# Another recording order for the first 1084 steps of a two-layer attention and feed-forward kernel

## The chip, the cores and the metric

The kernel runs on one core of a Trainium2 chip. The core has five engines, each with an instruction queue of its own that it works through in order: TensorE (PE in the profile; PEld are its weight loads), VectorE (DVE), ScalarE (ACT), GpSimd (POOL) and SyncE (SP), which here does nothing but issue DMAs. Engines wait for each other by semaphores. The metric is the device time of one execution, in microseconds.

## The reference

The program applies four layers to x (2048 tokens of 640 features), all with the same weights: attention, feed-forward, attention, feed-forward, each on a layer norm of x and each added to x.

```python
x = A_x
x = x + _A_ref(_layernorm(x, axis=-1), A_wq, A_wk, A_wv, A_wo, A_beta)
x = x + _B_ref(_layernorm(x, axis=-1), B_w1, B_w2)
x = x + _A_ref(_layernorm(x, axis=-1), A_wq, A_wk, A_wv, A_wo, A_beta)
x = x + _B_ref(_layernorm(x, axis=-1), B_w1, B_w2)
```

The attention has 32 heads of 20 features and works in 4 segments of 512 tokens. Within a segment it is causal softmax attention; beside it each head reads a memory matrix M, the sum of phi(k)^T v over the earlier segments, with phi(t) = t+1 for t > 0 and exp(t) otherwise. A gate per head mixes the two, and wo projects the result. The feed-forward is relu(x w1) w2 with 1728 hidden features.

## The kernel before

All weights and x stay on the core. The work is cut by layer and segment, and each kind of work is a Python generator (a stream) that yields steps one by one: an instruction, or a few that belong together, for one engine, with what they wait for. 39 streams are added at the end of the kernel, numbered from 0 in this order: scores, exps, causal, apply, free_v, turn_pair, divide, turn_o, two out_proj, two ln_b, fill, spill, combine, two phi_, two mem_read, turn_k, mem_write, first_sums, four first_one, first_ln_b, proj_ln, proj_first, two proj_one, proj_v, ffn, ffn_rest, store, warm_pe, consts, loads, late_loads. Some streams spawn small ones, mostly the copy that empties a PSUM bank.

The steps of segment 0, in the terms that are used below:

- `loads` brings x and the weights; `first_one` normalizes the first four tiles of 128 tokens and transposes them on TensorE; `proj_first`, `proj_one` (q and k, 512 columns a step) and `proj_v` (320 columns) project. A projection is five steps into one PSUM bank, at L774 or, in four column quarters, at L777. A copy (L981, L982, L1036) on VectorE or ScalarE empties the bank.
- `spill` (L1070) writes q and k to DRAM, `fill` (L1117) reads them back into `pad` with one head per group of 32 rows; four fills make the `pad` of two groups of four heads. The first pair comes straight from `stg` (L1097).
- `scores` (L1301) multiplies q and k in row groups. One step is a round, called SC0, SC1 and so on here; five rounds are the scores of eight heads. Each round ends in two exponentials on ScalarE (`exps`, L1365), which empty its banks; `causal` (L1377, GpSimd) masks them.
- `apply` multiplies the probabilities with v: at L1397 in column quarters (a value product), for groups 6 and 7 by token, in eight whole steps each (L1436). `turn_pair` transposes the result by DMA (L817), `divide` normalizes it, `out_proj` follows.
- `phi_` makes the features for the memory (L1144, L1146, L1147), `mem_write` (L1238) and `mem_read` (L1180) update and read it; `proj_ln` and `ln_b` are the layer norms (statistics at L795), whose results a DMA transposes (L817); `ffn` and `ffn_rest` (L1572) are the feed-forward; `late_loads` brings the later x, wo, w1 and w2.

Several of these TensorE steps exist in two forms, whole or in four column quarters. Going from row groups, whole or quarters to another of the three is called a change of form here.

What sets the order is a list scheduler (`Sched.run`). It keeps an estimated time for every engine, takes of all streams the step that could start first, shifted by priorities, by margins and by the table SHIFT, and records it: the instruction goes to the end of its engine's queue. So the order of recording is the program order of each queue. The scheduler also chooses the engine of a PSUM copy and the form of a TensorE step. 5068 steps are recorded.

## Time and profile before

| | before |
|---|---|
| median of 3 runs | 551.33 us (550.27 to 551.43) |
| profiled execution: span from the first to the last instruction | 549.3 us |
| TensorE busy | 539.8 us (98%) |
| VectorE busy | 427.8 us (78%) |
| ScalarE busy | 406.0 us (74%) |
| GpSimd busy | 195.7 us (36%) |
| mean granted TensorE clock | 1.000 |

The profile gives the profiled execution's time as its span; the runs' times also hold what lies around it, 2.0 us by the median. The page lists busy time by engine, the span in 40 slices, the DMA queues, the chain of work that ended last, and groups of instructions by line. Matmuls are pipelined: a matmul's duration in the profile is longer than the distance to the next one. A row of the timeline reads: start in us, length, engine, line, operation, result and operands, shapes, count, and in brackets idle time before it and what ended it.

### The profile page before, as it was taken

The numbers are of one execution on the slowest core, as the hardware profiler recorded it, in microseconds if no ns is written. First come the engines' busy times: TensorE is split into PE (matmuls) and PEld (weight loads), VectorE is DVE, ScalarE is ACT, GpSimd is POOL, SyncE is SP. The second block draws the span as 40 slices with busy tenths as digits, with TensorE's granted clock in tenths as the row PEclk, the third lists the DMA queues.
The fourth block names the chain that finished last, engine by engine and source line by source line (L and its number), as shares of the span: only waits on it lengthen the run. The fifth ranks groups of instructions, "written<-read, shape, count | busy, mean of one in ns | idle before, by whom it ended". The sixth has DMA issues, their size and how long they took to land.

```text
span 549.3 us, 20483 instructions
## 1 busy us (share of the span) xinstructions
PE 539.8 (98%) x9025; PEld 305.5 (56%) x9025; DVE 427.8 (78%) x1067; ACT 406.0 (74%) x516; POOL 195.7 (36%) x305
## 2 busy tenths in 40 slices
PE   7999999999999999999999999999999999999997
PEld 6543464455554546646556555564646654757656
DVE  4899999898999989898778858997899788417102
ACT  5699899789888987788888867897778787350130
POOL 5255444333453334443433423433333333201000
PEclk9999999999999999999999999999999999999999
DMA  8699979715384175438384743336246511541201
GB/s 270 165 198 253 245 158 223 221 44 116 89 165 98 40 180 77 75 68 120 47 212 93 116 116 93 58 69 104 50 139 130 117 32 22 106 63 33 71 2 51
DMA packets 133325, 62.20 MB, mean 113 GB/s; under 512 B 112116, under 2 KB 123124, under 8 KB 133236
## 3 DMA queue, kind: packets, MB, share of 16 engines
q1 hardware_dynamic: 132672, 60.36, 51.5%
q8 instruction: 71, 1.16, 0.9%
q10 hardware_dynamic: 564, 0.53, 0.4%
q14 instruction: 18, 0.15, 0.1%
HBM read 20.56 MB, written 12.85 MB: 61 GB/s over the span
## 4 chain that ended last, share of the span: by engine, by line
PE 88%; ACT 6%; DVE 2%; DMA 2%; SPq 1%; issue 0%
PE ps L774 35%; PE ps L777 35%; PE ps L1301 8%; PE ps L1397 6%; ACT PT L1365 5%; PE ps L1180 2%; DMA x_sb<-in_A_x_dram 1%; PE ps L1572 1%; PE ps L1238 1%; DMA pad<-scr 1%; SPq L602 1%; DVE xn_tok L841 0%; SPq L612 0%; DVE stats L795 0%; DVE x_sb L1614 0%; DVE o_sb L1491 0%
## 5 line engine op out<-in xcount | busy, mean ns | idle before, releaser
L1365 ACT ACTIVATE PT<-ps 128x1024 bf16<-128x1024 f32 x320 | 308.9, 1028 | 59.3 <-PE ps L1301 57.6
L1377 POOL TENSOR_SCALAR_AFFINE_SELECT PT<-PT 128x512 bf16<-128x512 bf16 x256 | 169.3, 679 | 241.1 <-ACT PT L1365 241.0
L777 PE MATMUL ps<-xnT,w_r 128*32 128x512 bf16 x1256 | 76.0, 379 | 0.0
L777 PE MATMUL ps<-w_r,hT 128*32 128x320 bf16 (+1 forms) x1764 | 67.8, 295 | 0.0
L1614 DVE TENSOR_TENSOR x_sb<-x_sb,ps 128x320 bf16<-128x320 bf16 (+1 forms) x65 | 30.7, 474 | 43.6 <-PE ps L777 38.7
L1301 PE MATMUL ps<-pad 20*128 20x512 bf16 (+3 forms) x1024 | 63.4, 301 | 1.2 <-ACT PT L1365 0.7
L774 PE MATMUL ps<-w_r,hT 128*128 128x320 bf16 x404 | 64.2, 300 | 0.0
L795 DVE BATCH_NORM_STATS2 stats<-x_sb 128x6 f32<-128x320 bf16 x124 | 55.0, 478 | 3.8 <-DMA x_sb<-in_A_x_dram 3.0
L777 PEld LDWEIGHTS ps<-w_r,hT 128*32 128x32 bf16 x1764 | 45.2, 97 | 12.6 <-issue 1.4
L1595 ACT ACTIVATE hT<-ps 128x512 bf16<-128x512 f32 x50 | 29.9, 599 | 29.0 <-PE ps L777 25.6
L774 PE MATMUL ps<-xnT,w_r 128*128 128x512 bf16 x206 | 50.8, 380 | 0.0
L774 PEld LDWEIGHTS ps<-w_r,hT 128*128 128x128 bf16 x404 | 37.6, 98 | 19.4 <-issue 4.9
L1301 PEld LDWEIGHTS ps<-pad 20*128 20x128 bf16 x1024 | 17.9, 92 | 52.9 <-issue 24.5
L777 PEld LDWEIGHTS ps<-xnT,w_r 128*32 128x32 bf16 x1256 | 31.6, 97 | 27.8 <-issue 2.0
L1519 DVE TENSOR_TENSOR x_sb<-x_sb,ps 128x320 bf16<-128x320 bf16 x64 | 29.7, 478 | 20.4 <-PE ps L777 16.0
L811 POOL TENSOR_TENSOR rstd<-lnU,mhalf 128x2 f32<-128x2 f32 (+2 forms) x27 | 21.1, 782 | 63.5 <-DVE lnU L807 60.4
L1407 DVE CAST otu<-ps 128x512 bf16<-128x512 f32 x52 | 35.6, 685 | 9.1 <-PE ps L1397 8.2
L1397 PE MATMUL ps<-PT,v_aug 128*21 128x128 bf16 (+3 forms) x896 | 40.3, 300 | 0.0
L1594 DVE TENSOR_SCALAR hT<-ps 128x512 bf16<-128x512 f32 x54 | 36.5, 681 | 1.7 <-PE ps L774 0.7
L1491 DVE TENSOR_TENSOR o_sb<-otk,rden 128x320 bf16<-128x320 bf16 x62 | 34.8, 588 | 0.5
L981 DVE CAST stg<-ps 128x512 bf16<-128x512 f32 (+1 forms) x37 | 24.7, 669 | 12.5 <-PE ps L774 6.3
L1146 ACT ACTIVATE stg<-stg 128x512 bf16<-128x512 bf16 x50 | 31.7, 635 | 2.0 <-DVE rtmp L1144 1.8
(118 smaller groups left out, 731.5 us busy)
## 6 DMA issues: line engine op xcount, KB each, us to landing
pad<-scr SPq DMA_DIRECT2D x124, 80.0 KB
scr<-stg SPq DMA_DIRECT2D x34, 256.0 KB, 2.5
out_dram<-x_sb SPq DMA_DIRECT2D x15, 160.0 KB, 1.9
w_r<-in_B_w_dram SPq DMA_DIRECT2D x10, 216.0 KB, 4.0
w_r<-in_B_w_dram SPq DMA_DIRECT2D x13, 160.0 KB, 2.8
x_sb<-in_A_x_dram SPq DMA_DIRECT2D x10, 160.0 KB, 3.2
scr<-w_r SPq DMA_DIRECT2D x5, 256.0 KB, 4.2
wv_r<-in_A_wv_dram SPq DMA_DIRECT2D x1, 800.0 KB, 9.7
```

Of the source, the lines that this page charges most:

```text
L774: return e.matmul(view(dst.ap, b), a, b, start=(k == 0), stop=(k == last))
L777: return e.matmul(view(dst.ap[rows], b), part, b, start=(k == 0), stop=(k == last))
L795: tk = yield dve(320, 1, lambda e, c2=c2: e.bn_stats(stats6[:, t, c2, :], x_sb[:, t, c2 * 320:(c2 + 1) * 320]), xt)
L1146: te = yield act(512, lambda e, q=q: e.activation(q, q, ACT.Exp), [tr] + p, psum=False)
L1301: fns.append([(lambda e, z=z, j=j, hh=hh, N=N, o=o, sl=sl, q=hh % 2: e.matmul(slot.ap[:, q, o:o + N], sl.ap[32 * hh:32 * hh + DH, z, 0, 12 ...
L1365: tx = yield act(1024, lambda e, dst=dst, src=src: e.activation(dst, src, ACT.Exp, scale=SCALE), sc + pw)
L1377: tm = yield pool(600.0, lambda e, reg=reg: e.affine_select(out=reg, in_=reg, pattern=[[0, 4], [1, 128]], compare_op=ALU.is_ge, fill=0.0, ...
L1397: fns.append((lambda e, OD, j=j, hh=hh: e.matmul(OD.ap[32 * hh:32 * hh + DH + 1, 128 * j:L], VAUG[vx(a, s)][:, j, 4 * g + hh, :], pt.ap[:, ...
L1407: te = yield evac(L, 1, lambda e: e.tensor_copy(dst, OD.ap), lambda e: e.activation(dst, OD.ap, ACT.Copy), [tk] + OTU[0].tks)
L1491: to = yield dve(320, 1, lambda e, z=z, dst=dst: e.tensor_tensor(dst, av[:, z, :, :, 0:DH], rd.ap[:, z].to_broadcast([128, NJ, 4, DH]), AL ...
L1594: th = yield evac(512, 1, lambda e: e.tensor_scalar(hT[:, dc, :], bk.ap[:, :], 0.0, None, ALU.max), lambda e: e.activation(hT[:, dc, :], b ...
L1614: ta = yield dve(n, 1, lambda e: e.tensor_tensor(x_sb[:, t, c0:c0 + n], x_sb[:, t, c0:c0 + n], bk.ap[:, 0:n], ALU.add), [tk], urgent=True)
```

## The change

The scheduler goes. The order is a list, ORDER, of 5068 numbers, one for each step: the number of the stream to take the next step from (40 more for the oldest unfinished small stream that it spawned), and 80 more for the other form, which is VectorE instead of ScalarE for a PSUM copy and column quarters instead of whole for a TensorE step that has both. "37*2" is 37 twice.

```diff
-LONE_NS = 300.0
...
-SHIFT = {
...
-HOLD_TOL = {"pe": 220.0, "act": 150.0, "dve": 200.0, "pool": 0.0, "sp": 0.0}
+ORDER = """
+37 36*2 35 37*2 35 36 21 36 21 37*2 36 21 35 21*2 26 21*3 22 21 26*2 22 26 22 21 37 22 37 26*2 28 66 108 23 28 37 23
+28 66 23 108 37 68 108*5 68 66 108*2 104 28*3 68 66 28*3 37 25 28 37 28 68 28*4 104 28 148 28 25 28*3 105 28 148 28*5
...
+"""
...
+        for word in ORDER.split():
+            code, _, count = word.partition("*")
+            for _ in range(int(count or 1)):
+                n, other = int(code) % 80, int(code) >= 80
+                st = tops[n] if n < 40 else next(x for x in self.kids[id(tops[n - 40])] if not x[3])
+                self._record(st, st[1].fn() if isinstance(st[1], Either) else st[1], other)
...
+        for sl in VA:
+            sl.free = False
...
+        PTS[0].free = False
...
-        def warm_mm(e):
-            return e.matmul(ps[:, 0, 0:128], warm_w, warm_w, start=True, stop=True)
+        def warm_mm(e, k=0):
+            return e.matmul(MISC[k // 4 % 4].ap[:, 128 * (k % 4):128 * (k % 4) + 128] if k < 16 else ps[:, 0, 0:128],
+                            warm_w, warm_w, start=True, stop=True)
...
             if t == 0:
-                yield pe(380.0, [(warm_mm, False) for _ in range(5)])
+                yield Acq([X])
+                yield pe(380.0, [(lambda e: warm_mm(e, 16), False) for _ in range(5)], X.tks)
+                X.release()
...
-                before = S.events.get(("filled", a, s - 2) if s > 1 else ("filled", a - 1, s + 2), [])
+                before = []
+                if (a, s) >= (0, 2):
+                    before = yield Need("filled", *divmod(NSEG * a + s - 2, NSEG))
```

Written as the same kind of list, the order of before differs from ORDER in 963 of the first 1084 places and in none of the 3984 behind them. The first 1084 steps take the same number of steps from every stream in both orders, so both have done the same work when the common part begins. They hold 37 rounds, SC0 to SC36. These are the TensorE steps that the two lists put between certain rounds, before / after:

| from, to | changes of form | 512-column steps | 320-column steps | by-token steps | other steps, the same in both |
|---|---|---|---|---|---|
| start to SC0 | 1 / 5 | 10 / 10 | 20 / 20 | 0 / 0 | 60 of 128 or 256 columns, warm-ups, 4 transposes |
| SC0 to SC5 | 10 / 10 | 23 / 22 | 40 / 40 | 0 / 0 | 5 rounds, 1 value product |
| SC5 to SC19 | 28 / 34 | 51 / 57 | 20 / 20 | 0 / 0 | 14 rounds, 5 value products, a memory write of 12 products in quarters |
| SC19 to SC20 | 2 / 2 | 13 / 5 | 3 / 5 | 16 / 8 | 1 round |
| SC20 to SC36 | 33 / 32 | 96 / 99 | 77 / 75 | 0 / 8 | 16 rounds, 6 value products, 5 memory reads, 1 ffn_rest, a memory write of 12 products in quarters, and one of 8 products: whole / in quarters |

Of the steps that exist whole and in quarters, 81 are in quarters before and 296 after. 26 PSUM copies are on ScalarE before and 31 after, 63 and 58 on VectorE. On SyncE's queue, around the transpose of pair 2 stand, before, three fills, the transpose, two loads, two spills, one fill; after, one spill, two fills, the transpose, two fills. Ahead of them two loads of w1 remain. The loads of w1 that stood there go behind segment 1's fills, and segment 3's layer norm and its transposes go back by some five rounds.

## The prediction

> **What bounds the kernel now.** I read the page first (shares of the span, slices), then the busy times by stretch, then the chain of waits, then TensorE's timeline around each gap.

> ```profile
> PE 539.8 (98%) x9025; PEld 305.5 (56%) x9025; DVE 427.8 (78%) x1067; ACT 406.0 (74%) x516; POOL 195.7 (36%) x305
> ...
> PE   7999999999999999999999999999999999999997
> ...
> PEclk9999999999999999999999999999999999999999
> ```

> TensorE (PE) is busy in every slice and its granted clock stays at the top digit, so nothing can be won from the clock. Only the first 1084 recorded steps change; before, they end with the 37th score round (SC36). So the question is when SC36 starts.

> ```profile
> 33.00:59.00 26.00, 24.38 (x341) 9.78 (x343) 25.52 (x61) 26.00 (x30) 15.88 (x24) 1.00 1.06 250
> ...
> 66.00:109.00 43.00, 43.00 (x611) 21.90 (x609) 40.30 (x97) 38.24 (x49) 17.13 (x27) 1.00 0.88 201
> ```

> The columns are the stretch and its length, then PE, PEld, DVE, ACT and POOL busy. From 33 to 59 us it is ScalarE (ACT) that has no free moment: 26.00 of 26. From 66 us on TensorE has none. Between the two the chain of waits (start, length, what) holds a fill of `pad`, that ends at SC20.

> ```profile
> 60.76 4.43 DMA pad<-scr
> ```

> **The price of a TensorE step.** A busy share overstates a pipelined TensorE, so I price steps by the distance from one start to the next.

> ```profile
> 52.16 1.25 PE L774 MATMUL ps<-hT,wq_r 128*128 128x512 bf16 x5 [0.27 <-DVE w_r L981]
> 53.34 0.40 PE L1301 MATMUL ps<-pad 20*128 20x384 bf16 x8
> 53.67 1.05 PE L777 MATMUL ps<-hT,wq_r 128*32 128x512 bf16 x16
> 54.55 0.72 PE L1397 MATMUL ps<-PT,w_r 128*21 128x512 bf16 x16
> 55.20 0.40 PE L1301 MATMUL ps<-pad 20*128 20x256 bf16 x8
> ```

> Line 774 is a whole step, line 777 the same step in four column quarters. Both cost alike at 512 columns: 16 quarters take 54.55-53.67 = 0.88 us, 0.22 a step; five whole steps take 1.18, which is 5 x 0.216 and 0.10 for the change of form to a round. The round takes 53.67-53.34 = 0.33, 0.235 and again 0.097 for the change back. A value product (line 1397) takes 0.65-0.10 = 0.54.

> ```profile
> 87.66 1.24 PE L774 MATMUL ps<-hT,wq_r 128*128 128x512 bf16 x5
> 88.83 0.72 PE L1397 MATMUL ps<-PT,v_aug 128*21 128x512 bf16 x16
> 89.38 0.73 PE L1572 MATMUL ps<-xnT,w_r 128*32 128x256 bf16 x20
> 90.05 0.40 PE L1301 MATMUL ps<-pad 20*128 20x384 bf16 x8
> ```

> Whole steps straight to quarters, with no round between, cost 1.17-5 x 0.216 = 0.09: as much as any other change. Quarters straight to whole is not in this trace; the nearest rows are these 0.09 and 0.10, and I take 0.097 for all. The rest of a feed-forward chunk (line 1572) takes 0.67-0.10 = 0.56.

> ```profile
> 59.24 1.18 PE L1436 MATMUL ps<-w_r,PT 128*128 128x21 bf16 x40
> 60.27 0.38 PE L774 MATMUL ps<-hT,wk_r 128*128 128x512 bf16 x1
> ...
> 68.63 0.68 PE L1238 MATMUL ps<-w_r,phk 128*128 128x147 bf16 x8
> 69.15 0.43 PE L774 MATMUL ps<-wv_r,hT 128*128 128x320 bf16 x2
> ...
> 83.06 0.65 PE L1238 MATMUL ps<-v_aug,phk 128*32 128x147 bf16 x48
> 83.52 0.84 PE L777 MATMUL ps<-hT,wq_r 128*32 128x512 bf16 x12
> ...
> 109.75 0.33 PE L1180 MATMUL ps<-BD,phs 128*128 128x147 bf16 x3
> 109.92 0.38 PE L774 MATMUL ps<-xnT,w_r 128*128 128x512 bf16 x1
> ```

> So eight by-token steps take 1.03; a memory write of eight whole products 0.52, and one of twelve in quarters only 0.46, since its quarters stream fewer columns (eight would be about 0.30); a memory read 0.17. A 320-column step is 0.136 (five of them and a change are 19.85-19.08 = 0.77 in the next fence).

> [...]

> **The count against the clock.** The first row gives the 320-column step; the others are the rounds SC0, SC5, SC19, SC20 and SC36.

> ```profile
> 19.08 0.84 PE L774 MATMUL ps<-wv_r,xnT 128*128 128x320 bf16 x5
> 19.85 0.39 PE L1301 MATMUL ps<-pad 20*128 20x512 bf16 x4
> ...
> 33.20 0.39 PE L1301 MATMUL ps<-pad 20*128 20x512 bf16 x4
> ...
> 58.91 0.40 PE L1301 MATMUL ps<-pad 20*128 20x384 bf16 x8
> ...
> 65.24 0.39 PE L1301 MATMUL ps<-pad 20*128 20x512 bf16 x4 [0.43 <-DMA pad<-scr]
> ...
> 109.19 0.40 PE L1301 MATMUL ps<-pad 20*128 20x384 bf16 x8
> ```

> With the step counts of the table in the section on the change, the work before is 13.09, 22.90, 5.68 and 43.79 us in the four stretches between these starts; they last 13.35, 25.71, 6.33 and 43.95. The idle time is the difference: 0.26, 2.81, 0.65, 0.16. That is all there is to win behind SC0. The work after is 12.88, 24.78, 3.21 and 44.87.

> **Part by part.**

> *Up to SC0.* The same work and four direct changes of form more, 0.39 us. Two of them stand ahead of the first multiply with wq, which waits for its load in either order, so they are hidden there.

> ```profile
> 9.00 0.45 PE L774 MATMUL ps<-xnT,wq_r 128*128 128x128 bf16 x5 [0.59 <-DMA wq_r<-in_A_wq_dram]
> ...
> 17.31 1.04 PE L774 MATMUL ps<-xnT,wq_r 128*128 128x512 bf16 x4 [0.44 <-DVE w_r L1036]
> ```

> That leaves +0.2. The gap at 17.31 is a PSUM bank that VectorE (DVE) frees late: the values of tile 0 stand behind statistics in its queue. The list moves both those copies to ScalarE, between its five `pad` issues; I take the gap as gone (0.6 us from step to step). Net -0.4; bounds +0.4 (gap stays, nothing hidden) and -0.7. Loads of x for segment 2 move behind spills, transposes and fills on SP's queue; their first reader is a statistic behind SC1, and those of the last two stand behind SC5.

> *SC0 to SC5.* One 512-column step fewer: -0.2; bounds -0.5 (no idle) and +0.3.

> *SC5 to SC19.* 28 exponentials bound it.

> ```profile
> 33.84 27.65 ACT L1365 ACTIVATE PT<-ps 128x1024 bf16<-128x1024 f32 x30
> 61.24 0.76 ACT L1146 ACTIVATE stg<-stg 128x512 bf16<-128x512 bf16 x1
> ```

> Thirty take 61.24-33.84 = 27.4, 0.914 each; 28 are 25.6. The list pulls one feature exponential (line 1146, about 0.5) into the stretch: 26.1, +0.4. TensorE gets 1.88 us more work there (six steps, six changes), which fills its idle time from 2.81 down to 1.3. Bounds: 24.8 (TensorE alone, -0.9) and 24.78+2.81 = 27.6 (it idles as before, +1.9). DVE, 25.52 busy of 26, has to keep up; statistics of segment 3 that stood in this stretch go behind it.

> *SC19 to SC20.* Nine 512-column steps less, of which eight had been put where TensorE had nothing else; and the second by-token product goes behind SC20. Work 3.21 instead of 5.68, if `pad` for segment 1 is there. Before, its last fill was issued at 60.76, behind two late weight loads and two spills, and landed 4.43 later.

> ```profile
> 55.53 1.17 SPq L1117 DMA_DIRECT2D pad<-scr  x3
> 56.74 1.93 SPq L817 DMA_TRANSPOSE otk<-otu  x1
> 58.71 1.06 SPq L643 DMA_DIRECT2D w_r<-in_B_w_dram  x2
> 59.81 0.91 SPq L1070 DMA_DIRECT2D scr<-w_r  x2
> 60.76 0.44 SPq L1117 DMA_DIRECT2D pad<-scr  x1
> ```

> After, two fills stand ahead of the transpose and two right behind it, with nothing between. If that transpose starts no later than at 55.5 (TensorE reaches its product a little earlier, and DVE copies it out at once), the last fill is issued near 57.5 and lands near 61.9; TensorE wants it at 19.4+13.1+26.1+3.2 = 61.8. I take 0.2 of waiting: 3.4, -2.9. Bounds 3.2 (-3.1) and 6.33 (as before, 0). [...]

> *SC20 to SC36.* 1.08 us more work: the by-token product (1.02) and three 512-column steps come in, two 320-column steps, a change and 0.22 of the memory write go out. TensorE is the bound and was idle 0.16; I allow 0.3, since the transposes for the feed-forward and the w1 loads now come later in SP's queue: 45.2, +1.25; bounds +1.1 and +1.9.

> *Without a price.* The warm-up multiplies write other PSUM banks: still 41, under the load of x. Slots that start as taken, and waits for events that had long come, issue nothing. Behind step 1084 the order is the same; its first need is w2, last issued here:

> ```profile
> 104.89 1.20 SPq L651 DMA_DIRECT2D w_r<-in_B_w_dram  x2
> ...
> 110.14 0.43 PE L774 MATMUL ps<-w_r,hT 128*128 128x320 bf16 x2
> ```

> The 15 pieces follow segment 1's last feature product on SP's queue; that product comes earlier too, and one fill joins them (0.4 us). If the cover fails, TensorE waits at SC36+0.95 for as long as they are late.

> **The sum.** -0.4-0.2+0.4-2.9+1.25 = -1.85: SC36 at 107.3 instead of 109.19, and the rest shifted by as much. The profiled execution's span is 549.3, so 547.4; the runs' median, 551.33, lies 2.0 above the span: 549.4.

> **The rivals.**
> 1. *TensorE idles from SC5 to SC19 as before* (2.81), since it waits there for DVE and not for work. For it: DVE is nearly as full there as ACT. Against: the statistics that leave. 27.6 instead of 26.1: 1.5 of the gain is lost, 550.9.
> 2. *Slower: the fill of `pad` for segment 1 stays late.* If SP issues its last fill at 60.76 as before, say because the transpose ahead waits, SC20 stays at 65.2, TensorE has already spent its cover (5.68 is now 3.21), and SC36 is at 65.2+45.2 = 110.4: 552.6. It decides from SC20 at 64.0 on (no gain) and 65.1 (slower by 0.2%). For it: one queue in order, and a transpose of 1.93 between. Against: the four issues that leave the place.
> 3. *More gain*: SC5 to SC19 is bound by TensorE's 24.8, the exponentials starting earlier: 1.3 better, 548.1.

> **How the numbers follow.** Forecast 0.52 (its own range 548.7 to 550.2), rival 1 0.20, rival 2 0.13, rival 3 0.12, a wait nowhere seen 0.03. 0.2% is 1.1 us, about what can be told from no change. Faster takes the forecast, rival 3 and a fifth of rival 1: 0.68; same the rest of rival 1 and a little: 0.17; slower 0.15. The range reaches from rival 3 to beyond rival 1, 548.0 to 551.8.

> **What would show it.** SC0 near 19.4; SC5 to SC19 near 26 us, with ACT full; SC20 near 62; 45.2 us from there to SC36 with TensorE never idle; 83 changes of form. Wrong it would be if SC20 is later than 64, if TensorE waits for the second pair's `pad` at SC5 (a spill now stands between its fills), for `hT` (segment 2's transposes) near SC17, or for w2 behind SC36.

## The result: slower by 0.9%, and where the profile puts it

The changed kernel takes 555.7 us (median of 553.73, 555.57, 555.82 and 557.48); the kernel before, on the same chip, 550.8. The ratio is 1.0086, with a 95% interval of 1.0067 to 1.0106. Timed again later it was 1.0069 (1.0046 to 1.0093). The forecast was 549.4. The profiled execution took 553.73 with a span of 551.6: 2.3 us more than the one before (549.3). It was the fastest of the four; in a second pair of profiled executions the times differ by 4.2 us.

Starts of the rounds, in us (profiled execution of each kernel, TensorE's timeline):

| | before | after | difference | forecast of the difference |
|---|---|---|---|---|
| SC0 | 19.85 | 17.96 | -1.89 | -0.4 |
| SC0 to SC5 | 13.35 | 13.71 | +0.36 | -0.2 |
| SC5 to SC19 | 25.71 | 26.46 | +0.75 | +0.4 |
| SC19 to SC20 | 6.33 | 3.34 | -2.99 | -2.9 |
| SC20 to SC36 | 43.95 | 49.08 | +5.13 | +1.25 |
| SC36 to SC159, the last round | 360.39 | 361.37 | +0.98 | 0 |

At SC20 the changed kernel is 3.77 us ahead, more than the 3.1 forecast, but 1.89 of it, at SC0, is luck of this profile: a second pair of profiles, described below, has SC20 only 1.13 us earlier. From SC0 to SC20 the gain is 1.88 us here and 1.23 in the second pair, where 2.7 was forecast. Behind SC20 the changed kernel loses 5.1 us in 16 rounds, and 1.0 far behind them, where both orders are the same. Busy times of the stretch from SC20 to SC36 (columns as in the prediction), first of the changed kernel:

```profile
61.47:110.55 49.08, 46.05 (x1030) 24.55 (x1030) 41.91 (x109) 40.94 (x55) 18.56 (x30) 1.00 0.97 207
```

and of the kernel before:

```profile
65.24:109.19 43.95, 43.95 (x616) 22.21 (x617) 41.16 (x101) 38.57 (x49) 17.32 (x27) 1.00 0.89 202
```

TensorE, never idle there before, is idle for 3 us, and busy for 2.1 more. Its timeline has the gaps as idle time in brackets (start, length, then what the profile takes for the releaser):

```profile
70.39 0.86 PE L748 MATMUL ps<-wo_r,oT 128*32 128x320 bf16 x20 [1.21 <-ACT PT L1334]
...
90.33 0.40 PE L748 MATMUL ps<-xnT,w_r 128*32 128x512 bf16 x4 [1.01 <-issue]
...
94.30 1.05 PE L748 MATMUL ps<-xnT,w_r 128*32 128x512 bf16 x16 [0.56 <-DVE otu L1376]
...
381.88 0.82 PE L745 MATMUL ps<-xnT,wq_r 128*128 128x512 bf16 x3 [0.74 <-DMA xnT<-xn_tok]
```

In the first row the named releaser had been done for 0.7 us, and the second names none; in the third the named copy had itself waited. Each of the four is a transpose that landed late: of `oT` (issued 65.22, landed 70.30) for the output projection, of the feed-forward's second `xnT` (84.97, 90.24), of `otk` (88.77, 93.53; VectorE waits for it with the copy that frees a bank), and of the second layer's `xnT` (376.19, 381.84). The bracket counts from the modelled end of the matmul before. A 512-column matmul lasts 0.38 us in the rows and the next can start 0.22 behind it, so counted from start to start, as the prediction counts, a wait is some 0.16 us longer than its bracket (0.07 behind a round): 1.38, 1.18, 0.73 and 0.90 here. Waits outside brackets are counted so below, unless the text says otherwise.

SP's queue around them:

```profile
65.22 1.35 SPq L788 DMA_TRANSPOSE oT<-o_sb  x1
66.62 0.68 SPq L613 DMA_DIRECT2D w_r<-in_B_w_dram  x1
67.36 2.02 SPq L788 DMA_TRANSPOSE oT<-o_sb  x1
...
82.25 0.43 SPq L613 DMA_DIRECT2D w_r<-in_B_w_dram  x1
82.72 5.44 SPq L788 DMA_TRANSPOSE xnT<-xn_tok  x2
88.21 0.52 SPq L1085 DMA_DIRECT2D pad<-scr  x1
88.77 1.24 SPq L788 DMA_TRANSPOSE otk<-otu  x1
```

w1 loads stand between and ahead of the transposes, where the order before had none. That was the first theory; it did not hold. The DMA view of the stretch around the feed-forward's transposes shows what else differs (40 slices of 0.21 us, a digit for the busy share; then queues with packets, MB, share; then issues with the median us to landing). The changed kernel:

```profile
DMA  9879999989989994039800000199999999449999
...
q8 instruction: 1, 0.02, 1.4%
q14 instruction: 1, 0.01, 0.4%
...
xnT<-xn_tok SPq DMA_TRANSPOSE x2, 5.8
```

The kernel before, over the same length:

```profile
DMA  0000019999999900000499999999999999999999
...
q8 instruction: 1, 0.02, 0.7%
...
xnT<-xn_tok SPq DMA_TRANSPOSE x2, 4.1
```

In both a packet of kind "instruction" moves on queue q8, and soon behind it stands a hole of five slices, 1.1 us, in which next to nothing moves though a transpose is under way. Before, the packet came at 84.0, with only the first transpose under way (issued 81.54): that one was late too, 4.73 us, but TensorE did not wait for it, and the second, issued at 85.76 behind the hole, took 3.53. After, it came at 85.3, with both under way, and both were late (6.27 and 5.27). The pages' queue tables count these packets; before:

```profile
q8 instruction: 71, 1.16, 0.9%
...
q14 instruction: 18, 0.15, 0.1%
```

after:

```profile
PE 540.8 (98%) x9655; PEld 307.2 (56%) x9655; DVE 425.8 (77%) x1062; ACT 408.8 (74%) x521; POOL 195.1 (35%) x305
...
q8 instruction: 76, 1.25, 0.9%
...
q14 instruction: 17, 0.14, 0.1%
```

### The profile page after: what moved, and what is told of

The parts are those of the page before. It is cut to its first block, busy times and chain, and to the rows that moved or that the text cites. A ratio compares the mean times of both kernels' runs of the same rounds, so it can differ in the third digit from the quotient of the medians.

```text
span 551.6 us, 21742 instructions
## 1 busy us (share of the span) xinstructions
PE 540.8 (98%) x9655; PEld 307.2 (56%) x9655; DVE 425.8 (77%) x1062; ACT 408.8 (74%) x521; POOL 195.1 (35%) x305
## 3 DMA queue, kind: packets, MB, share of 16 engines
q8 instruction: 76, 1.25, 0.9%
## 4 chain that ended last, share of the span: by engine, by line
PE 83%; DVE 10%; DMA 3%; ACT 2%; SPq 1%; issue 0%; POOL 0%
PE ps L748 37%; PE ps L745 29%; PE ps L1272 8%; PE ps L1366 6%; DVE stats L766 2%; PE ps L1148 2%; DVE xn_tok L812 1%; DMA x_sb<-in_A_x_dram 1%; ACT PT L1334 1%; DMA xnT<-xn_tok 1%; DMA otk<-otu 1%; PE ps L1206 1%; DVE phs L1115 1%; DVE o_sb L1460 1%; PE ps L1541 1%; DVE x_sb L1488 1%
## 5 line engine op out<-in xcount | busy, mean ns | idle before, releaser
L748 PE MATMUL ps<-xnT,w_r 128*32 128x512 bf16 x1380 | 83.9, 380 | 1.6 <-issue 1.0
L748 PEld LDWEIGHTS ps<-xnT,w_r 128*32 128x32 bf16 x1380 | 34.7, 97 | 32.6 <-issue 3.8
L745 PEld LDWEIGHTS ps<-w_r,hT 128*128 128x128 bf16 x404 | 37.6, 98 | 19.4 <-issue 4.9
L1272 PEld LDWEIGHTS ps<-pad 20*128 20x128 bf16 x1024 | 17.9, 92 | 50.8 <-issue 25.8
L782 POOL TENSOR_TENSOR rstd<-lnU,mhalf 128x2 f32<-128x2 f32 (+2 forms) x27 | 21.5, 795 | 63.4 <-DVE lnU L778 60.4
L745 PE MATMUL ps<-xnT,w_r 128*128 128x512 bf16 x175 | 43.6, 380 | 0.0
L1376 DVE CAST otu<-ps 128x512 bf16<-128x512 f32 x50 | 34.3, 685 | 10.1 <-PE ps L1366 7.9
```

Source lines behind the costliest of these rows:

```text
L745: return e.matmul(view(dst.ap, b), a, b, start=(k == 0), stop=(k == last))
L748: return e.matmul(view(dst.ap[rows], b), part, b, start=(k == 0), stop=(k == last))
L1272: fns.append([(lambda e, z=z, j=j, hh=hh, N=N, o=o, sl=sl, q=hh % 2: e.matmul(slot.ap[:, q, o:o + N], sl.ap[32 * hh:32 * hh + DH, z, 0, 12 ...
L1376: te = yield evac(L, 1, lambda e: e.tensor_copy(dst, OD.ap), lambda e: e.activation(dst, OD.ap, ACT.Copy), [tk] + OTU[0].tks)
```

## The experiments

The list edits are shown by the names of the steps they move (streams of the kernel), not as numbers. Ratios are to runs of the kernel before on the same chip, with 95% intervals.

### Are the w1 loads or the order of SP's queue to blame?

`w1_gathered`:

```diff
 turn_o (oT, first transpose)
-late_loads w1 piece 4
 turn_o (second)
 turn_k segment 1
-late_loads w1 pieces 5, 6, 7
+late_loads w1 pieces 4 to 10
 proj_ln segment 3 (two transposes)
-late_loads w1 pieces 8, 9, 10
 ln_b (the feed-forward's two transposes)
```

> The changed kernel with one group moved in its list: the four w1 loads that stand between and just ahead of the transposes (one between the two oT transposes, three spread ahead of the feed-forward's xnT transposes) are issued in one run with the other three, behind the keys' transpose that follows oT (near 71.7 us). Nothing else moves. Theory (transposes stand behind w1 loads in SP's queue and in the DMA queues): the feed-forward's second xnT transpose is issued in about 1.4 us instead of 3.2 and lands near 88.8 instead of 90.24, TensorE's stalls of 1.19 us at 89.0 and 0.73 us at 93.35 go, the 1.38 us at 68.8 stays; SC36 near 108.7 instead of 110.55, the span near 549.7 instead of 551.6. Rival (the later part of the new list is slow by its form, its quartered steps or its vector work, not by these transposes): SC36 within 0.4 us of 110.55 and the span within 0.5 us of 551.6.

Measured: 555.61 us, 1.0076 (1.0055 to 1.0097), SC36 at 113.09, which neither text has. One part of the theory held: the feed-forward's second transpose landed 3.52 us behind its issue. But that issue came at 87.64 instead of 84.97: segment 3's transposes stood behind the loads and were late, they held a buffer that VectorE's normalization waited 1.85 us for, and TensorE waited longer than before. Behind that wait the granted clock fell as well (0.5 for 3.41 us, last section). One cure made another wait.

`w1_and_values_first`, over it:

```diff
+proj_v segment 2, tile 1, right half (5 steps); proj_part segment 2 (1 step); two memory-write copies
 out_proj tile 0 (10 steps)
-the same steps
```

> The kernel w1_gathered with one more move: five value-projection steps and one step of the segment-2 projection (0.9 us of TensorE work), with the two vector copies that free their bank, are recorded ahead of the first output-projection step instead of behind it. Theory: TensorE has this work to do while the oT transpose lands, so the 1.38 us stall at 68.8 falls to about 0.4 us, SC36 near 107.7, the span near 548.8. Rival (what bounds this stretch is not TensorE's wait for oT but a chain that the wait only shows, such as the vector engine's): the stall shrinks and comes back as another before SC36, which stays where w1_gathered has it.

Measured: 555.15 us, 1.0073 (1.0053 to 1.0093). The wait for oT shrank to 0.48 us, and 0.63 and 1.31 us appeared later. SC20 to SC36 took 48.27 us, 2.5 less than in the profile of w1_gathered, so its SC36 did not stay, but no less than in the changed kernel (49.08; 48.21 in the second profile), and the times of the three do not differ beyond their intervals. Giving TensorE work to do gained nothing over the changed kernel.

`w1_in_the_gap`:

```diff
-late_loads w1 pieces 4 to 10 (from their places in the changed kernel)
+late_loads w1 pieces 4 to 7
 turn_o (both)
 turn_k segment 1
+late_loads w1 pieces 8 to 10
 ln_b (two transposes)
```

(with the six steps and two copies of `w1_and_values_first` moved likewise)

> The changed kernel with the seven put-off w1 loads in other places: four of them issued in the gap of SP's queue ahead of oT (61.7 to 65.2 us, in which the queue issues nothing), three directly behind the keys' transpose near 71.7, none between the two oT transposes and none ahead of the feed-forward's two; and, as in w1_and_values_first, 0.9 us of projections ahead of the output projection. Theory (the debt of the new list can be paid in that gap; w1 loads in the DMA queues ahead of a transpose are what makes it late): oT lands no later than 71 us, the feed-forward's transposes at or before 89.0, TensorE's idle between SC20 and SC36 under 1.5 us instead of 4.2, SC36 near 107.8, the time 1.5 to 2 us under that of the changed kernel and no slower than before. Rival (what was put off behind SC20 costs TensorE the same wherever it stands): four loads ahead of oT delay it by 1.5 to 2.5 us, the stall moves there, SC36 at 110 or later.

Measured: 555.43 us, 1.0082 (1.006 to 1.0103). The feed-forward's transposes landed in 3.7 us and its wait was gone; oT took 5.5. SC20 to SC36: 48.31. The rival's number came, but neither text explains it: with or without loads in front, oT had taken 5.07, 5.28, 5.07 and 5.5 us in the changed kernel and these three.

`w1_last_three_behind` and `w1_behind_values_first` put w1 pieces 8 to 10 behind the feed-forward's transposes, and piece 4 behind the keys' transpose; the second also has the six steps and two copies of `w1_and_values_first` moved:

```diff
-late_loads w1 piece 4 (between the two of turn_o)
 turn_k segment 1
+late_loads w1 piece 4
...
-late_loads w1 pieces 8, 9, 10
 ln_b (two transposes)
 turn_pair 4; turn_k segment 1
+late_loads w1 pieces 8, 9, 10
```

> The changed kernel with four w1 loads moved: the one between the two oT transposes goes behind the keys' transpose, and the last three, which only the second half of the feed-forward's hidden units needs, go behind the feed-forward's two xnT transposes and the two that follow. Theory (a chain bounds SC20 to SC36: oT's transpose is issued, 18.8 to 20.4 us later the feed-forward's second xnT transpose, it lands, and 19.9 to 20.9 us of TensorE work follow up to SC36; loads ahead of it in the DMA queues make the landing 5.1 to 5.3 us instead of 3.5 to 3.7): with no w1 load ahead the second xnT transpose lands in 3.5 to 3.9 us, and SC36 comes 43.3 us behind oT's issue within 0.5, instead of 45.3 and 44.5 in the two profiles of the changed kernel; TensorE's stalls of 1.2 to 1.6 us near 89 and 0.7 us near 94 go. Time: 1.2 to 1.9 us less than the changed kernel. Rival (the landing is late for the pad fills and the keys' transposes, not for w1): landing over 4.8 us, SC36 44.5 us or more behind oT's issue.

> The kernel w1_last_three_behind with the 0.9 us of projections put ahead of the output projection, as in w1_and_values_first. Theory (the chain bounds, TensorE only waits for it): the stall for oT near 69 us shrinks by 0.5 to 0.9 us, and SC36 stays 43.3 us behind oT's issue within 0.5, so nothing is won over w1_last_three_behind. Rival (TensorE's idle time is itself the loss): SC36 comes 0.6 us or more sooner behind oT's issue than in w1_last_three_behind.

Measured: 560.61 us, 1.0168 (1.0146 to 1.0189), and 559.14, 1.0138 (1.0117 to 1.0159). I had overlooked that ffn_rest, here behind the feed-forward's first eight 512-column steps, reads the last 64 columns of w1 and so needs all of it:

```profile
96.68 0.58 PE L1541 MATMUL ps<-xnT,w_r 128*32 128x256 bf16 x12 [3.67 <-DMA w_r<-in_B_w_dram]
```

So their times say nothing on the theory. Their landings do: in the first the second `xnT` landed in 3.53 us, in the second in 5.53, with the same queue and no w1 load just ahead in either. A transpose can be late without them. (A 16 KB fetch began 0.4 us ahead of the issue in the first, 2.0 us behind it in the second.)

### Which part of the list loses?

`new_to_21_then_old`: the new list up to SC21, then what is left in the old order. `old_to_19_then_new`: the other way round, from SC19.

```diff
-ORDER = new list
+ORDER = new list up to SC21 + the steps not yet taken, in the old order        (new_to_21_then_old)
+ORDER = old order up to SC19 + the steps not yet taken, in the new list's order (old_to_19_then_new)
```

> The new list up to round 21, then all steps that are left in the order of the kernel before. Theory (the gain up to SC20 is real, and what loses it is the new order of SP's queue behind it): SC20 near 61.5 as in the changed kernel, idle of TensorE between SC20 and SC36 under 0.8 us, SC36 near 105.5 to 106.3 (109.19 less 3.8, and some of the 1.1 us for change of form saved), the span near 546, faster than before by 0.6%. Rival (another chain, loads or the vector engine, holds SC36 near 109 whatever TensorE does before): TensorE idles 3 us or more between SC20 and SC36, SC36 at 108.5 or later, the span at 549 or more.

> The order of the kernel before up to round 19, then all steps that are left in the new order. Theory (the transposes of the new order are late only because TensorE arrives 3.8 us sooner): the pad fills for segment 1 stay late, SC20 near 65.2, TensorE's stalls for oT and the feed-forward's xnT are gone or under 0.5 us together, SC36 near 110.4 (109.19 plus 1.1 us of more work), the span near 550.5. Rival (the new order is slow behind round 20 by itself, its w1 loads among the transposes, whenever it starts): the idle of about 4 us between SC20 and SC36 is there again, SC36 at 112.5 or later, the span at 552.7 or more.

Measured: 554.4 us, 1.0064 (1.0041 to 1.0088), and 553.59, 1.0054 (1.0035 to 1.0072). The first came out near its rival's numbers (SC36 at 112.33), by a cause that neither text names: seven w1 loads and the put-off statistics of segment 3 came at once, oT was issued at 70.48 instead of 65.22, SC22 came at 73.49. That part of the gain up to SC20 is a debt: work that the old list has done by then and the new one has not. The second: SC20 came at 63.42, not 65.2, and SC36 at 109.02, with 45.60 us between. TensorE's idle time in between was 0.07 us by the busy times. So the new order behind SC20 does not bring its idle time wherever it stands. But this kernel, too, lost 1.0 us near 381 us.

### Form and order apart

`quarters_in_old_order` keeps the old order and takes the new form for 224 steps; `new_order_old_form` is the reverse.

```diff
-ORDER = new list
+ORDER = old order, each step in the form that the new list gives it (quarters_in_old_order)
+ORDER = new list, each step in the form that the old order gives it (new_order_old_form)
```

> The order of the kernel before, each TensorE step of it in the form that it has in the changed kernel (224 steps change form, 215 net become quartered); no step moves. By the prices of the prediction this order then has 94 changes of form instead of 74 and 1.7 us more of counted TensorE work up to SC36. If form alone makes the changed kernel slower: SC36 near 110.9 (109.19 plus 1.7) and the time 1.5 us or more above before. Theory (form costs little, since TensorE has idle time up to SC20 that takes it up; the loss lies behind SC20 in transposes): what lies ahead of SC20 is hidden, SC20 within 0.3 us of 65.2 and SC36 at most 0.6 us above 109.19.

> The order of the changed kernel, each TensorE step in the form that it has in the kernel before (the same 224 steps change back). By the prices of the prediction this order has 103 changes of form instead of 83 and 2.2 us more of counted TensorE work up to SC36, of which 0.8 us less up to SC20, 1.3 us more from there to SC28, 1.65 us more from SC28 to SC36. Theory (chain): the 1.3 us lie in TensorE's idle time and cost nothing, the 1.65 us behind the last transpose count in full: SC36 46 to 47 us behind oT's issue, the time 1.2 to 2 us over the changed kernel. Rival (the quartered form slows this stretch by more than its changes of form, so the old form is better here): SC36 less than 44.5 us behind oT's issue, the time under that of the changed kernel.

Measured: 554.78 us, 1.0069 (1.005 to 1.0089), and 553.72, 1.0041 (1.0025 to 1.0057). Form alone, with no step moved, costs about as much as the whole change. My theory for it fell: SC0 to SC20 was as before (45.46, the extra work hidden), but SC20 to SC36 took 46.05 instead of 43.95, and hardly by late transposes (oT landed in 3.50 us, the second `xnT` in 4.57). More than half of it is one wait in the middle of a memory write:

```profile
83.76 0.53 PE L1206 MATMUL ps<-v_aug,phk 128*32 128x147 bf16 x34
85.33 0.26 PE L1206 MATMUL ps<-v_aug,phk 128*32 128x42 bf16 x13 [1.04 <-issue]
```

The trace names no semaphore that TensorE waits for here. Over all 20 profiles, from SC0 on, only four of its gaps above 0.03 us are without one: this, 0.78 us in before_code_64 (at 256.97), 0.28 in w1_behind_values_first (80.56) and 0.20 in before_code_40 (254.61). All four stand 193 to 195 TensorE instructions behind a multiple of 256 in the trace, and a 16 KB fetch had begun 2.4 to 2.6 us before each of them ended. So I take it that in these places TensorE waited for its own code; no record names that wait.

In the reverse kernel TensorE's gaps are gone, in the same order and with the same w1 loads among the transposes:

```profile
62.47:111.15 48.68, 48.52 (x659) 22.63 (x660) 41.91 (x109) 41.14 (x55) 18.72 (x30) 1.00 0.89 211
```

It pays in changes of form (103; SC20 to SC36 is no shorter), yet oT landed in 3.38 us and the second `xnT` in 3.60. Both texts missed: SC36 came 44.92 us behind oT's issue, and the time lies under the changed kernel's (1.0086, 1.0069), not over it. In its DMA view from 66 to 72 us no instruction packet moves:

```profile
q1 hardware_dynamic: 3156, 0.98, 85.9%
...
oT<-o_sb SPq DMA_TRANSPOSE x2, 3.7
```

while the changed kernel has one from 65 to 71, at 68.2:

```profile
q1 hardware_dynamic: 2496, 0.82, 86.6%
q8 instruction: 1, 0.02, 0.9%
...
oT<-o_sb SPq DMA_TRANSPOSE x2, 4.8
```

### Both kernels again

Nothing is edited: the profiles of both kernels are taken a second time.

> The kernel before once more, for its profile. Theory (the 0.9 us at 381 us of the changed kernel comes from its order): the transposes at the start of the second layer land in time again, no stall there and SC20 near 65.2. Rival (that stall comes and goes with the landing time of a transpose, 4.4 to 5.7 us in the profiles so far, in any order): a stall of up to 1 us between SC128 and SC132, and SC0 up to 0.8 us off 19.85.

> The changed kernel once more, for its profile and its times. Theory: TensorE's stalls for oT near 69 us and for the feed-forward's xnT near 89 us are there again within 0.5 us, SC20 to SC36 take 49.1 us within 0.5; SC0 between 17.9 and 18.9, as the kernels with the same list up to there showed. Rival (the profiled execution was an accident): SC20 to SC36 take less than 47 us.

Measured: 550.17 us (one time), SC0 at 19.34, SC20 at 64.19, SC20 to SC36 44.18, no wait near 381. And 554.82 us, 1.0069: SC0 at 19.45, SC20 to SC36 48.21, waits of 1.6 and 0.7 us near 89 and 94 and of 0.8 near 381, but none for oT. So the loss behind SC20 repeats, 0.9 us smaller than the stated 49.1 and so beyond its bound, and so does the wait near 381, which had seemed chance. The early SC0 does not: over eight executions that have the new list, its form and the same warm-up up to there, it lay between 17.96 and 19.52, 18.9 on the mean, against 19.85, 19.34 and 19.21 (19.5 on the mean) with the old list: a gain of 0.6, near the 0.4 forecast.

### Does the place of TensorE's code decide?

Over 20 profiled executions I sorted the transposes of each kind by whether a 16 KB fetch began while they were under way (from 1 us behind the issue to 0.3 us ahead of the landing); those that met a fetch of 8 KB, on queue q14, are left out. Median us from issue to landing, number in brackets:

| transpose | no fetch | one 16 KB fetch |
|---|---|---|
| oT | 3.54 (154) | 5.04 (104) |
| xnT | 3.55 (283) | 4.72 (180) |
| otk | 3.11 (486) | 4.57 (113) |
| phk | 3.66 (121) | 4.51 (51) |

A transpose that is late for another reason has more time to meet a fetch, so the table alone proves nothing. A window that does not depend on the landing does better. With a fetch that began 1.0 to 2.5 us behind the issue, oT took 4.89 us (42 of them), xnT 4.74 (62), otk 4.53 (77), phk 4.58 (17); with none from 2 us ahead of the issue to 4.5 behind it, 3.53 (65), 3.40 (101), 3.11 (144), 3.64 (19). And 31 transposes stand in both groups, each the same transpose of the program, by its number in the order of issue, in different executions: 30 of them are slower with the fetch, one is alike, and the median of the differences is 1.1 us.

The next seven runs move the fetches without a change to any other step: the warm-up at the start, 41 multiplies of 128 columns, becomes more multiplies of fewer columns. Here 64 more (24 and 48 likewise, with 65 and 89 in all):

```diff
-[(lambda e, k=k: warm_mm(e, k), k == 40) for k in range(41)]
+[(lambda e, k=k: warm_mm(e, min(k, 20), 32), k == 104) for k in range(105)]
```

Order and form of all other steps stay. 64 multiplies and their weight loads are 128 instructions, half a packet. One thing besides the code does change: in the five kernels with 32 columns TensorE is slower behind the warm-up, until 9.5 to 11.6 us (five multiplies of 128 columns last 0.74 us in their rows, 0.44 in the kernel before). SC0 comes at 19.3 and 19.7 us in the two of them with the old list, as without, and at 19.4 to 20.3 in the three with the new one (18.0 to 19.5 without), so their times ahead of SC20 are no clean test.

> The changed kernel with 65 warm-up matmuls of 32 columns in place of 41 of 128 columns: 24 matmuls with their weight loads, 3 KB of TensorE code, more ahead of everything, nothing else changed. Theory (a 16 KB fetch of TensorE's code stops a transpose that it meets for 1 to 1.5 us): all fetches come about 1.0 us earlier against the work (5.5 us times 3 of 16 KB); from 3.0 and 20.1 us behind oT's issue in the changed kernel they move to 2.0 and 19.1: oT is still met (over 4.5 us), the feed-forward's first transpose too, its second no more (3.5 to 3.9 us instead of 5.1 to 5.3); SC36 43.5 us behind oT's issue within 0.7. Rival (what stands in the queues makes the transposes late): landing times as in the changed kernel, SC36 44.5 us or more behind oT's issue.

> The same with 89 warm-up matmuls, 48 more, 6 KB of code. Theory: the fetches come about 2.1 us earlier, at 0.9 and 18 us behind oT's issue: oT hardly met (under 4.2 us), the feed-forward's second transpose free (3.5 to 3.9 us); SC36 43.3 us behind oT's issue within 0.6. Rival: as in the changed kernel, 44.5 us or more.

> The same with 105 warm-up matmuls, 64 more, 8 KB of code (half a fetch). Theory: the fetches come about 2.8 us earlier, at 0.2, 17.3 and 23.4 us behind oT's issue, between the transposes: oT and both of the feed-forward's land in 3.4 to 3.9 us, TensorE's idle between SC20 and SC36 is 2 us or less instead of 3.4 to 4.2, SC36 43.0 us behind oT's issue within 0.5, and this part of the time is 1.5 to 2.3 us shorter than in the changed kernel (the rest of the kernel meets fetches anew, which is not worked out). Rival: as in the changed kernel.

> The kernel before with 105 warm-up matmuls of 32 columns in place of 41 of 128: 8 KB more code ahead of everything. Theory: its fetches, which lie at 17.8 to 18.3 and 25.2 to 25.4 us behind oT's issue, between the transposes, come about 3.6 us earlier, the second of them at 21.7 us, where it meets the feed-forward's second transpose (issued 18.8 to 19.6, landed 22.8 to 23.2): it lands in 4.6 us or more instead of 3.5 to 4.0, and SC36 comes 43.8 us or more behind oT's issue instead of 42.7 and 43.0. Rival: nothing moves, SC36 42.9 us behind oT's issue within 0.3.

| kernel | us | ratio, 95% interval | SC0 to SC20 | SC20 to SC36 | SC36 to SC159 | oT, first and second: landing | feed-forward's xnT, first and second: landing | SC36 behind oT's issue |
|---|---|---|---|---|---|---|---|---|
| before (two profiles) | 550.8 | | 45.39, 44.84 | 43.95, 44.18 | 360.39, 360.53 | 3.5, 3.6; 3.5, 3.7 | 4.7, 3.5; 3.4, 4.0 | 43.0, 42.7 |
| before_code_64 | 555.98 | 1.0085 (1.0061 to 1.0108) | 46.78 | 45.12 | 362.93 | 3.5, 5.4 | 3.6, 4.7 | 44.0 |
| after (two profiles) | 555.7, 554.8 | 1.0086, 1.0069 | 43.51, 43.61 | 49.08, 48.21 | 361.37, 361.60 | 5.1, 4.5; 3.7, 4.6 | 6.3, 5.3; 6.0, 5.1 | 45.3, 44.5 |
| after_code_24 | 554.67 | 1.0073 (1.0051 to 1.0095) | 43.70 | 46.95 | 360.96 | 5.1, 4.6 | 4.3, 3.6 | 43.8 |
| after_code_48 | 554.23 | 1.0063 (1.0038 to 1.0088) | 42.72 | 47.83 | 360.72 | 4.3, 3.7 | 5.3, 5.6 | 44.1 |
| after_code_64 | 554.85 | 1.0064 (1.004 to 1.0087) | 43.23 | 48.11 | 362.21 | 3.9, 5.4 | 5.3, 5.5 | 44.4 |

The kernel before, with 8 KB of dead code ahead of it, is as slow as the changed kernel. Its SC0 is the same (19.32), so the other warm-up as such does not delay it up to there. The wait forecast for it came, at the first step that reads the feed-forward's `xnT`, though in part by luck: the fetch began 19.6 us behind oT's issue, 0.2 us behind that of the second transpose, not at 21.7:

```profile
91.42 0.73 PE L1572 MATMUL ps<-xnT,w_r 128*32 128x256 bf16 x20 [0.89 <-issue]
```

More of the kind came elsewhere: its gaps ahead of 137.29 (0.66 us, for oT) and 157.04 (0.76, for xnT) are not in the profiles of the kernel before, and in both places a fetch had begun 1.9 to 3.4 us behind the issue of the transposes. With the wait for code at 256.97 (0.94 from start to start) they are the 2.4 us by which SC36 to SC159 is longer. What SC0 to SC20 lost, 1.4 to 1.9 us, was not followed up.

For the changed kernel the theory's numbers came once in three. In after_code_24 oT was late, the second transpose took 3.64 us, and SC36 came at 43.8, as forecast, with the fetches at 3.1 and 18.2 us behind oT's issue instead of 2.0 and 19.1: the second of them 2.1 us ahead of the second transpose's issue. after_code_48 and after_code_64 missed: a fetch came 22.4 and 21.5 us behind oT's issue, where the first text has none and the second has 23.4; there it met the second transpose, which was late (5.6, 5.5), and SC36 came 44.1 and 44.4 us behind oT's issue, above the theory's bounds and just under the rival's 44.5. So the theory of what a fetch does held, and my working of where the fetches fall did not. No place tried was without any meeting: with 8 or 9 fetches between SC20 and SC36, one every 6 us, some of the transposes on the way always met one. That fits the changed kernel's ratios, 1.0063 to 1.0086 at all of them, while the kernel before, with 5 or 6 fetches there, ranges over 0.85%.

Three last runs: the place behind SC36, with 10 more multiplies of 96 columns, and two more places for the kernel before, with 20 more of 64 columns and 40 more of 32:

```diff
-[(warm_mm, k == 40) for k in range(41)]
+[(lambda e: warm_mm(e, 64), k == 60) for k in range(61)]
```

> The changed kernel with 51 warm-up matmuls of 96 columns in place of 41 of 128: 20 TensorE instructions more, so that behind round 36 its code crosses 16 KB one instruction from where that of the kernel before does. Theory (fetches decide which transposes are late): the stall near 381 us, 0.8 to 0.9 us in the changed kernel, is under 0.3 us, and the rounds from SC36 to SC159 take what they take in the kernel before (360.4 to 360.5 us) within 0.2, instead of 361.4 to 361.6; up to SC36 the fetches move by only 0.4 us, so most of that loss stays. Time: 0.6 to 1.0 us less than the changed kernel. Rival (what the new prefix leaves behind in queues and buffers makes that transpose late): the stall stays at 0.6 us or more.

> The kernel before with 61 warm-up matmuls of 64 columns in place of 41 of 128, 40 TensorE instructions more. Theory: its fetches come 1.1 us earlier behind SC20, at about 17 and 24 us behind oT's issue: the feed-forward's second transpose stays free (4.0 us or less), SC36 within 0.5 us of 42.9 us behind oT's issue. What the other transposes of the kernel meet is not worked out: the time lies between that of the kernel before and 0.9% above it, and each us over it is found as a stall for a transpose with a fetch in its way. Rival (the place of the code means nothing): the time is that of the kernel before within 0.2%.

> The same with 81 warm-up matmuls of 32 columns, 80 instructions more than the kernel before. Theory: fetches about 2.3 us earlier behind SC20, near 15.7 and 22.9 us behind oT's issue, the second just as the feed-forward's second transpose lands (22.8 to 23.2): 3.5 to 4.7 us for it; the time between that of the kernel before and 0.9% above it. Rival: the time is that of the kernel before within 0.2%.

Measured: 553.74 us, 1.0063 (1.0041 to 1.0086); 551.54, 1.0013 (0.9995 to 1.0031); 553.03, 1.0046 (1.0025 to 1.0067). before_code_40 is slower than the kernel before by its other warm-up alone; before_code_20 is not told from it. In both the feed-forward's second transpose was free (3.65 and 3.56 us). In before_code_20 the first one met its fetch and took 4.95, which I had not worked out, and SC36 came 43.7 us behind oT's issue, 0.3 beyond the stated bound.

after_code_10 missed, and its rival's number came: SC36 to SC159 took 361.10 us, and the wait near 381 us was still 0.67, though its TensorE fetch was as far from SC128 as in the kernel before (0.35 us ahead; 0.46 and 0.38 before). The DMA view shows a difference. The changed kernel from 374 to 383 us:

```profile
DMA  0000000019999999990000099990005985856846
...
q8 instruction: 1, 0.02, 0.6%
q14 instruction: 1, 0.01, 0.3%
...
xnT<-xn_tok SPq DMA_TRANSPOSE x2, 5.3
```

The kernel before, from 372.7 to 381.7:

```profile
DMA  0000000039999999000199999964856757300000
...
q8 instruction: 1, 0.02, 0.7%
...
xnT<-xn_tok SPq DMA_TRANSPOSE x2, 4.4
```

after_code_48, from 374.5 to 383.5:

```profile
DMA  0000000005999999999999900992426856750000
...
q14 instruction: 1, 0.01, 0.2%
...
xnT<-xn_tok SPq DMA_TRANSPOSE x2, 3.9
```

There are two fetches: the second is 8 KB on queue q14, not TensorE's. In the changed kernel the second hole stands where it moves. In all ten profiles that have the new list behind SC21 and code shifted by 20 instructions at most (whole packets aside), the 16 KB fetch falls between 0.6 us ahead of SC128 and 0.3 behind it, the 8 KB one 2.0 to 2.3 us behind SC128, and the wait is 0.64 to 1.0 us. With the old list behind SC21 (before twice, quarters_in_old_order, new_to_21_then_old) the 16 KB fetch falls in the same place, the 8 KB one 3.2 to 3.5 us ahead of SC128, outside the transposes, and there is no wait. In after_code_48 and after_code_64 the 16 KB fetch is out of the way and the 8 KB one alone makes no wait either, though it also lies 1 us nearer to SC128. So it probably takes both, which is not shown, and I had moved the wrong one. Whose code the 8 KB are is argued, not shown: VectorE has 1086 instructions after and 1094 before, and 8 of its instructions, some 0.7 us each here, are the 5.6 us by which this fetch came later; when it begins, 828 of VectorE's instructions have begun before, and 835 after.

## Why the prediction was wrong

**Right.** The changed kernel reaches SC20 earlier, by the steps named: no late fill of `pad` (rival 2 did not come: SC20 at 61.47 to 63.3 in all executions of the list), SC19 to SC20 shorter by 2.99 us (forecast 2.9), TensorE's idle time between SC5 and SC19, by the prediction's count, down from 2.8 to 1.7 (rival 1 did not come). Sizes off: SC0, where 1.89 in this profile is 0.6 on the mean; SC0 to SC5, +0.36 instead of -0.2; SC5 to SC19, +0.75 instead of +0.4; SC19 to SC20, -2.49 in the second pair. A slip without effect: the 512-column steps that leave SC19 to SC20 are eight, not nine, and the sum of 3.21 was made with eight.

**Wrong, first step.** "TensorE is the bound and was idle 0.16; I allow 0.3, since the transposes for the feed-forward and the w1 loads now come later in SP's queue." It was idle for 3.0 us by the busy times, and for 4.0 counted from start to start. The sum for SC20 to SC36 was forecast at +1.25 with bounds of 1.1 and 1.9; it is +5.13, and +4.0 in the second pair of profiles. I looked for lateness in the queue's order, where the row "82.72 5.44" seems to confirm it; five kernels with other orders of that queue were no faster. The transposes are late where fetches of code meet them: the same transpose of the program is slower with one than without (30 of 31, by 1.1 us at the median). The reverse kernel, with the same queue and the old amount of code, has 0.16 us of idle time.

**Wrong, the step beneath it.** "Both cost alike at 512 columns." On TensorE they do (0.22 us each in the rows of the prediction). What I left out of the price of a quartered step is its code: four multiplies and four weight loads instead of one of each, 384 bytes more at the 64 an instruction that 16 KB / 256 gives. 630 such multiplies make five fetches of 16 KB, all in the first 110 us, where the critical transposes are. Form alone in the old order made the kernel 0.69% slower, there with TensorE's own wait for code, 1.2 us, as the largest piece. TensorE itself seldom waited for it: four times in 20 profiles, for 0.20 to 1.04 us by the brackets. The larger cost is on the transposes: with a fetch that began 1.0 to 2.5 us behind the issue they took 0.9 to 1.4 us longer, by the medians of the four kinds.

**Wrong, the last step.** "The rest shifted by as much." Behind SC36 the order is the same and the work is the same, but the place of the code is not: the wait near 381 us costs 0.9, by the fetches near it, as far as the comparison above goes. I had treated an equal order as an equal program.

**What stays open.** Whether the new order would beat the old one with no fetch in the way: no run had that. Of the +5.13 us, 1.1 is counted work and 4.0 waiting, both from start to start (1.1 and 3.1 of the second pair's +4.0), so little is left over; but 0.7 of the 4.0 is in small waits whose causes were not sought. Why transposes are slower with a fetch is not shown, only that they are.

## What to carry to other kernels

Count instructions as well as engine time: here a form that costs the same on TensorE but takes four times the instructions brought five more 16 KB fetches of code for 630 more multiplies, transposes under way with one took 0.9 to 1.4 us longer, and TensorE itself, as I read its four gaps, waited for 0.20 to 1.04 us. Before a change of order is called slower or faster by under 1%, shift the code by some dead instructions at the start and time both kernels at several places; here the unchanged kernel moved by 0.85% that way. When a transpose is late, look at the instruction queues in the DMA view before the order of its own queue.

## What the runs showed of the hardware

Beside the fetches: some long waits of TensorE cost twice. In w1_gathered it waited 1.88 us near 87 us (all waits of this section by their brackets):

```profile
89.03 0.32 PE L748 MATMUL ps<-wv_r,hT 128*32 128x320 bf16 x4 [1.88 <-DVE stg L950]
```

and the granted clock (the column behind POOL's) fell for the next microseconds, with TensorE busy all the time:

```profile
88.00:90.00 2.00, 0.97 (x24) 0.42 (x28) 2.00 (x5) 0.79 (x2) 0.87 (x2) 0.83 1.01 216
90.00:92.00 2.00, 2.00 (x24) 0.80 (x20) 1.05 (x4) 2.00 (x3) 0.27 (x1) 0.50 0.90 187
92.00:94.00 2.00, 2.00 (x56) 1.02 (x52) 1.17 (x3) 0.59 (x2) 0.37 (x1) 0.81 1.06 246
```

The clock record has 0.5 for 3.41 us there, which is 1.7 us of work lost. The same 3.41 us came with the waits of 2.62, 3.67 and 3.58 us in new_to_21_then_old, w1_last_three_behind and w1_behind_values_first. It did not come behind the gaps of 1.0 to 1.6 us in the changed kernel's profiles and after_code_10, nor behind one of 1.90 us near 91 us in after_code_64. So the length of the wait alone does not decide.
